# Window attention then top-1 experts: interleaved slots that begin one step later, with routing pieces at other places

## The chip, the cores and the metric

The kernel runs on one core of a Trainium2 chip. The metric is the device time of one execution in microseconds (us). Five engines work side by side, each in its own program order: PE (matrix products, transposes among them), DVE (vector work), ACT (activations and copies), POOL (GpSimd) and SP (which here only issues DMAs). They wait for each other by semaphores.

## What is computed

```python
# q, k, v: 8 batches, 8 heads, 576 positions, 64 wide; window 64; 8 experts, 512 -> 1024 -> 512
scores = q @ k.T / 8, kept where 0 <= i - j < 64
x = softmax(scores) @ v                    # (4608, 512)
logits = x @ w_gate                        # (4608, 8)
e = argmax(logits); gate = softmax(logits)[e]
out = gate * (relu(x @ w1[e]) @ w2[e])     # each row by its one expert
```

All in float32. The expert products are made as three products of split operands (`hi*hi`, `hi*lo`, `lo*hi`), so each weight and each row block is first split into a high and a low part.

## The kernel before

The 4608 rows are 36 tiles of 128. One attention step `i` makes `scores(i)` and, for tiles begun in earlier steps, the exponentials (`exps`, ACT), the transposes of them (`transp`, PE into the bank `t_b`), their copy (`evac`, ACT), the masked halves (`apart`, two products on POOL), the product with v (`values`, PE into `x_b`), the division (`shares`, DVE, then a DMA of the rows to the DRAM table `xs`), the transposes of the finished rows (`rows_t`, PE) and their copy (`cols_t`, ACT tile `xT`). For every second tile, `logits` and in the step after it `by_token` make the router's logits in a spare part of `x_b`; DVE reads them (`lgT`, `lgs`).

Tiles are routed in rounds of 8, 6, 8 and 14 (`ROUNDS`). After a round's last logits, `route` queues eight stages `s1` to `s8` (`slow`); `s4` is the rank product on PE, the others are DVE work. Then come the pieces (`puts`): one `hot_row` a tile, six parts of a table (`here`, `said`), the table's product (`gathered`, PE, and `read`, DVE: `eidx`, `egate`), and the fetches of rows (`early_rows`, indirect DMAs issued by POOL into the three buffers `xg`). Round 1 gives the rows of experts 0 and 1, round 2 those of experts 2 to 7.

The program has four stages:

1. Steps 0 to `TURN - 1` (27 of them), attention alone, written out in one fixed order per step. The last two also turn the two row blocks of expert 0 (`turn`: PE transposes into `m_b`, ACT `xeh`, DVE `xel`).
2. Slots `TURN` to 37: one attention step each, with eight turns (`next(early)`) of the first expert passes between its parts. `first_passes` gives each of the 8 experts two blocks of 128 rows; one of its eight units `j` is 12 products into the hidden bank `m_b` (L280, one turn), with `hh` (ACT), `hl` (DVE) and the splitting of a further weight piece (`whi` ACT, `wlo` DVE), and 6 products of the unit before (L242, `flush`, the other turn). During units 3 and 6 the next expert's rows are turned (units 6 and 7 in expert 1). A slot so holds four units, and two slots an expert.
3. What is left of `early` after the slots, 40 turns; after each of them one step of `steps()`: the last logits, the last round's `s1` to `s8`, the plan of the later passes (`plan`: DVE chains, then the product `want` on PE from `diag`, then the six parts of the big table), `table` (`gathered` with 36 products), and the first fetches. In this stage the hidden banks are `t_b` and `m_b` in turn, and `turn` uses `s_b`.
4. The later passes, two of 384 rows and then nine of 256, and a conditional tail.

PSUM banks are shared: in the slots `t_b` takes `transp`, `rows_t` and `turn` one after the other, each of which waits until ACT (and DVE) have read the one before; `m_b` is the only hidden bank, so the products of unit `j + 1` wait for `hl` of unit `j`.

Of the kernel before, what the change touches and what calls it, by code (L numbers as in the profile page):

```python
# [58 lines left out]
RND = float(1 << 23)  # L59
LOADW = 12  # L60
AHEAD = 2
SPLIT = 16
TURN = 27


CO = {}
# [41 lines left out]
def window_attention_then_top1_moe(ctx: ExitStack, tc: tile.TileContext, qkv, wall, wg, cst, out):  # L108
# [328 lines left out]
    def cols_t(n):  # L437
        q = n % 2
        if q == 0:
            rs_["xT"] = wk.tile([P, 4, 2, P], F32, name="xT", bufs=2)  # L440
        xT = rs_["xT"]
        nc.scalar.copy(out=xT[:, :, q], in_=xps.pop(n).rearrange("p (k t) -> p k t", k=4))
        if q == 1:
            nt = ROUNDS[rs_["round"]]
            if rs_["chunk"] == 0:
                rs_["lgs"] = rt.tile([P, nt, E], F32, name="lgs")
            lgT = rt.tile([P, 2, P], F32, name="lgT")
            c0 = rs_["chunk"]
            rs_["chunk"] += 2
            last = rs_["chunk"] == nt  # L450
            args = nt, rs_["lgs"], rs_["tile0"], rs_["round"]
            lgs = rs_["lgs"]

            def first():
                logits(xT, lgT)

            def second():
                by_token(lgT, lgs[:, c0:c0 + 2], args if last else None)

            rs_["fast"].extend([first, second])  # L460
            if last:
                rs_["tile0"] += nt
                rs_["chunk"] = 0
                rs_["round"] += 1
# [12 lines left out]


    slow, puts = deque(), deque()
    rs_ = {"round": 0, "chunk": 0, "tile0": 0, "fast": deque(), "read": None}  # L480

    def logits(xT, dst):
# [169 lines left out]
    def plan():  # L652
        cnt = small("cnt")
        nc.vector.tensor_tensor(out=cnt, in0=base, in1=cc("ebase"), op=ALU.subtract)
        yield
        nb = floor_of("nb", cnt, 1.0 / P, 127.0 / 256)
        left = small("left")
        nc.vector.tensor_tensor(out=left, in0=nb, in1=cc("st0"), op=ALU.subtract)
        half = floor_of("half", left, 0.5, -0.25)
        odd = stt("odd", half, -2.0, left, ALU.mult, ALU.add)  # L660
        pref = stt("pref", half, 1.0, odd, ALU.is_ge, ALU.mult)
        yield

        ch1 = stt("ch1", running("rk1", pref), float(NWIDE), pref, ALU.is_le, ALU.mult)
        rest = small("rest")
        ts(rest, pref, -1.0, ALU.mult, 1.0, ALU.add)
        sum1 = small("sum1", 1)
        nc.vector.tensor_reduce(out=sum1, in_=ch1, op=ALU.add, axis=AX.X)
        yield
        ok = small("ok")  # L670
        ts(ok, running("rk2", rest), sum1, ALU.add, float(NWIDE), ALU.is_le)
        ch = small("ch")
        nc.vector.tensor_tensor(out=ch, in0=ok, in1=rest, op=ALU.mult)
        nc.vector.tensor_tensor(out=ch, in0=ch, in1=ch1, op=ALU.add)
        yield
        wide = running("wide", ch)
        l2 = stt("l2", ch, float(-WIDE), left, ALU.mult, ALU.add)
        ts(l2, l2, 0.0, ALU.max)
        end = running("end", floor_of("ns", l2, 0.5, 0.25))
        yield  # L680
        nc.vector.tensor_copy(out=tot_sb, in_=end[:, E - 1:E])

        ends = small("ends")
        nc.vector.tensor_tensor(out=ends, in0=wide, in1=end, op=ALU.subtract)
        ends = stt("ends2", ends, cc("kind"), end, ALU.mult, ALU.add)
        yield
        le = small("le")
        ts(le, ends, cc("scol"), ALU.is_le)
        es = small("es", 1)
        nc.vector.tensor_reduce(out=es, in_=le, op=ALU.add, axis=AX.X)  # L690
        yield
        e7 = small("e7", 1)
        ts(e7, es, float(E - 1), ALU.min)
        nc.vector.tensor_copy(out=es_sb, in_=e7)
        nc.vector.tensor_tensor(out=le, in0=le, in1=ends, op=ALU.mult)
        sta = small("sta", 1)
        nc.vector.tensor_reduce(out=sta, in_=le, op=ALU.max, axis=AX.X)
        yield
        begin = stt("begin", ch, cc("three"), cc("st0"), ALU.mult, ALU.add)
        mine = stt("mine", cc("eid"), es, begin, ALU.is_equal, ALU.mult)  # L700
        b0 = small("b0", 1)
        nc.vector.tensor_reduce(out=b0, in_=mine, op=ALU.add, axis=AX.X)
        yield
        blk = small("blk", 1)
        nc.vector.tensor_tensor(out=blk, in0=cc("scol"), in1=sta, op=ALU.subtract)
        blk = stt("blk2", blk, 2.0, cc("ucol"), ALU.mult, ALU.add, 1)
        blk = stt("blk3", es, float(REG), blk, ALU.mult, ALU.add, 1)
        nc.vector.tensor_tensor(out=blk, in0=blk, in1=b0, op=ALU.add)
        ts(blk, blk, NONE, ALU.min)
        yield  # L710

        diag = rt.tile([P, NM], F32, name="diag", bufs=1)
        ts(diag, ident[:, 0:NM], blk, ALU.mult)
        wp = s_b[0][:, 1, 0:NM]
        nc.tensor.matmul(wp, lhsT=ones_f[0:NM], rhs=diag[0:NM], start=True, stop=True)
        want = xn.tile([P, NM], F32, name="want")
        nc.vector.tensor_copy(out=want, in_=wp)
        yield
        keep["want"] = want
        for b in parts(xn, want[:, 0:NMA], NT, NMA):  # L720
            keep["said"] = b
            yield
# [66 lines left out]
    def do_ranks():  # L789
        if slow and slow[0][0]:  # L790
            slow.popleft()[1]()
# [3 lines left out]
            if puts and not slow and (tables or not puts[0][0]):  # L795
                puts.popleft()[1]()

    def do_fast():
        if rs_["fast"]:
            rs_["fast"].popleft()()  # L800
            rs_["read"]()
            rs_["read"] = None

# [14 lines left out]
    def slots(i):  # L818

        if i == TURN:  # L820
            cols_t(i - 5)
            evac(i - 2)
            apart(i - 2)
            turned.append(i - 4)
        each(exps, i - 1)
        back = bool(turned)
        values_shares(i - 3 if i == TURN else i - 2)
        if back:
            move()
        next(early)  # L830
        do_puts(1, False)
        next(early)

        each(transp, i - 1)
        each(evac, i - 1)
        each(apart, i - 1)
        if rs_["fast"]:
            do_fast()
        next(early)
        do_slow(3)  # L840
        do_puts(2)
        next(early)

        move()
        do_ranks()
        next(early)
        do_slow(3)
        do_puts(2)
        next(early)

        if rs_["fast"] and rs_["fast"][0].__name__ == "first":
            do_fast()
        if i == TURN:
            values_shares(i - 2)
        each(scores, i)
        each(folded, i)
        each(largest, i)
        next(early)
        do_slow(1)
        do_puts(1)  # L860
        next(early)

    with tc.manual_schedule():
        for i in range(TURN):
            for c in range(RING, 2 * NS):

                if i == (c - RING + 1) // 2 + 4:
                    nc.sync.dma_start(out=ring[:, c % RING], in_=qkv[c // UC, :, c % UC])
            if i == LOADW:
                ew[0] = Weights(0)  # L870
            if i == SPLIT:
                stream.extend([ew[0].split_(pieces) for _ in range(AHEAD)])
            each(exps, i - 1)
            each(evac, i - 2)
            each(apart, i - 2)
            each(cols_t, i - 5)
            if TURN - 2 <= i < TURN:
                turn(xg[0], i - TURN + 2, xe[0], m_b)
            each(scores, i)
            each(folded, i)  # L880
            each(largest, i)
            each(values, i - 3)
            if rs_["fast"]:
                rs_["fast"].popleft()()
            do_ranks()
            each(rows_t, i - 4)
            each(transp, i - 1)
            each(shares, i - 3)
            if rs_["read"]:
                rs_["read"]()  # L890
                rs_["read"] = None
            do_slow(3)
            do_puts(4)
            if pieces:
                pieces.popleft()()
# [12 lines left out]
        spare["at"] = s_b[0]  # L908

        def steps():  # L910
            do_fast()
            yield
            while slow:
                slow.popleft()[1]()
                yield
            for _ in plan():
                do_puts(1)
                yield
            while puts:
                do_puts(2)  # L920
                yield
            table(0, NMA)
            while keep["turned"] < EARLY - 1:
                yield
            get(0)
            yield
            open_weights(0)
            get(1)
# [71 lines left out]
```

## Time and profile before

| | |
|---|---|
| median of 3 runs | 698.92 us (695.08 to 699.53) |
| profiled execution, its own time | 692.68 us |
| its span | 690.9 us |
| stage 1 (to about 118, with the turned rows to 141) | PE 92.61 of 118 us, then 14.84 of 23 us |
| slots (about 141 to 320) | PE 166.49 of 179 us |
| rest of the first passes (320 to 404) | PE 74.29 of 84 us |
| later passes (404 to 691) | PE 278.31 of 287 us |
| PE, DVE, ACT, POOL over the span | 91%, 63%, 52%, 28% busy |

A busy PE includes the stretches at which the clock granted to it was half, in which the same product takes about twice as long. The granted clock stands in its own column of the views by stretch.

### The profile page before, as it was taken

What the parts mean: (1) busy time and instruction counts of PE and PEld (TensorE: products, weight loads), DVE (VectorE), ACT (ScalarE), POOL (GpSimd) and SP (SyncE); (2) the same over time, 40 slices, a digit from 0 to 9 for tenths busy, and PEclk for the clock granted to TensorE, in tenths of its full rate; (3) what the DMA queues carried; (4) which work ended last, traced back from release to release, by engine and by line L of the source; (5) the groups of instructions that cost most, each with busy time, mean ns of one, the idle gap of its engine ahead of it and who ended that gap; (6) DMA issues with size and microseconds to landing.
All of it is one profiled execution on the core that took longest, in us unless ns stands there. A gap on an engine that the chain in (4) does not pass through costs nothing.

```text
span 690.9 us, 16970 instructions
## 1 busy us (share of the span) xinstructions
PE 626.5 (91%) x6998; PEld 553.4 (80%) x6998; DVE 434.0 (63%) x821; ACT 358.8 (52%) x760; POOL 190.8 (28%) x159
## 2 busy tenths in 40 slices
PE   4897887668996999999987999999999999999995
PEld 3776676557885888887877989999999999999994
DVE  3786989456784857675697554444565556555651
ACT  3664565354653665655444453435655565555551
POOL 2664554531223443311011621112212212110011
PEclk9999999899998999999999999999999999999998
DMA  9788675556372846546454764445666667655520
GB/s 356 248 266 288 243 237 190 187 200 228 126 267 69 300 144 240 189 149 229 132 199 145 246 225 148 161 153 167 219 228 218 212 214 240 210 208 189 205 92 32
DMA packets 32087, 138.13 MB, mean 200 GB/s; under 512 B 4603, under 2 KB 4987, under 8 KB 21633
## 3 DMA queue, kind: packets, MB, share of 16 engines
q1 hardware_dynamic: 25600, 118.08, 49.3%
q0 software_dynamic: 6400, 18.88, 8.1%
q8 instruction: 57, 0.93, 0.5%
q14 instruction: 30, 0.24, 0.1%
HBM read 119.12 MB, written 19.92 MB: 201 GB/s over the span
## 4 chain that ended last, share of the span: by engine, by line
PE 72%; DVE 15%; issue 5%; ACT 4%; DMA 2%; POOL 0%; SPq 0%; ACTq 0%; POOLq 0%; DVEq 0%
PE m_b L280 20%; PE s_b L242 18%; PE t_b L280 11%; PE x_b L242 10%; PE s_b L362 3%; PE x_b L418 3%; DVE wlo L220 3%; DVE mx L377 2%; PE s_b L179 2%; ACT whi L219 1%; DVE s_b L373 1%; ACT pf L388 1%; PE t_b L393 1%; DVE mxs L380 1%; DVE xrow L428 1%
## 5 line engine op out<-in xcount | busy, mean ns | idle before, releaser
L220 DVE TENSOR_TENSOR wlo<-raw,whi 128x1024 fp32r<-128x1024 f32 (+1 forms) x158 | 198.4, 1256 | 142.4 <-ACT whi L219 138.1
L219 ACT CAST whi<-raw 128x1024 fp32r<-128x1024 f32 (+1 forms) x158 | 160.7, 1017 | 75.9 <-PE s_b L242 40.1
L404 POOL TENSOR_TENSOR pm<-tsb,cs 128x512 f32<-128x512 f32 x72 | 91.5, 1293 | 129.8 <-ACT tsb L397 127.2
L286 ACT ACTIVATE hh<-m_b 128x256 fp32r<-128x256 f32 (+1 forms) x98 | 38.6, 394 | 94.0 <-PE m_b L280 94.0
L388 ACT ACTIVATE pf<-s_b,mxs 128x64 f32<-128x64 f32 x288 | 62.9, 333 | 45.2 <-DVE den L424 22.8
L242 PE MATMUL s_b<-whi,hh 128*128 128x512 f32 x208 | 82.4, 396 | 0.0
L242 PE MATMUL s_b<-wlo,hh 128*128 128x512 f32 x208 | 81.9, 394 | 0.0
L242 PE MATMUL s_b<-whi,hl 128*128 128x512 f32 x208 | 81.6, 393 | 0.0
L250 POOL DMA_INDIRECT out<-ys,idx_sb x24 | 30.0, 1251 | 148.9 <-ACT ys L249 145.0
L280 PE MATMUL m_b<-xeh,whi 128*128 128x256 f32 x216 | 65.4, 303 | 0.3 <-DVE hl L287 0.3
L287 DVE SCALAR_TENSOR_TENSOR hl<-m_b,hh 128x256 fp32r<-128x256 f32 (+1 forms) x98 | 42.2, 431 | 37.1 <-ACT hh L286 36.9
L418 PE MATMUL x_b<-ring,pm 64*64 64x65 f32 x2176 | 45.9, 229 | 19.2 <-DVE lgs L471 8.3
L418 PEld LDWEIGHTS x_b<-ring,pm 64*64 64x64 f32 x2176 | 41.6, 141 | 25.4 <-issue 24.6
L280 PE MATMUL m_b<-xel,whi 128*128 128x256 f32 x216 | 61.2, 283 | 0.0
L280 PE MATMUL m_b<-xeh,wlo 128*128 128x256 f32 x216 | 61.1, 283 | 0.0
L280 PE MATMUL t_b<-xh,whi 128*128 128x256 f32 (+1 forms) x176 | 52.3, 297 | 0.0
L280 PE MATMUL m_b<-xh,whi 128*128 128x256 f32 (+1 forms) x176 | 52.3, 297 | 0.0
L168 POOL DMA_INDIRECT xg<-xs,idx_sb x24 | 26.2, 1092 | 93.9 <-PE s_b L179 87.9
L280 PE MATMUL t_b<-xl,whi 128*128 128x256 f32 (+1 forms) x176 | 51.4, 292 | 0.8 <-DVE xl L182 0.8
L280 PE MATMUL m_b<-xh,wlo 128*128 128x256 f32 (+1 forms) x176 | 51.6, 293 | 0.0
L280 PE MATMUL t_b<-xh,wlo 128*128 128x256 f32 (+1 forms) x176 | 51.6, 293 | 0.0
L280 PE MATMUL m_b<-xl,whi 128*128 128x256 f32 (+1 forms) x176 | 51.4, 292 | 0.0
(187 smaller groups left out, 1350.3 us busy)
## 6 DMA issues: line engine op xcount, KB each, us to landing
raw<-wall SPq DMA_DIRECT2D x76, 1024.0 KB, 5.2
ring<-qkv SPq DMA_DIRECT2D x55, 386.0 KB, 4.5
xs<-xrow SPq DMA_DIRECT2D x36, 256.0 KB, 2.3
ring<-qkv SPq DMA_DIRECT2D x5, 1158.0 KB, 11.6
ring<-qkv SPq DMA_DIRECT2D x1, 512.0 KB, 4.0
cs<-cst SPq DMA_DIRECT2D x1, 404.5 KB, 4.5
xg<-xs,idx_sb POOLq DMA_INDIRECT x24, 4.1
out<-ys,idx_sb POOLq DMA_INDIRECT x24, 3.1
```

Of the source, the lines that this page charges most:

```text
L168: nc.gpsimd.indirect_dma_start(out=t[:, u], out_offset=None, in_=xs[0:rows], in_offset=bass.IndirectOffsetOnAxis(ap=ix, axis=0), bounds_ch ...
L219: nc.scalar.copy(out=hi[:, s], in_=raw[:, s])
L220: nc.vector.tensor_tensor(out=lo[:, s], in0=raw[:, s], in1=hi[:, s], op=ALU.subtract)
L242: nc.tensor.matmul(y, lhsT=x[:, us], rhs=w[:, C:], start=(j == 0 and m == 0), stop=(j == NJ - 1 and m == 2))
L250: ins = nc.gpsimd.indirect_dma_start(out=out, out_offset=bass.IndirectOffsetOnAxis(ap=ix, axis=0), in_=ys, in_offset=None, bounds_check=N ...
L280: nc.tensor.matmul(hp[:, 0:w], lhsT=a[:, ks], rhs=x[:, kk, 0:w], start=(m == 0), stop=(m == 11))
L286: nc.scalar.activation(out=hh[:, 0:w], in_=hp[:, 0:w], func=AF.Relu)
L287: nc.vector.scalar_tensor_tensor(out=hl[:, 0:w], in0=hp[:, 0:w], scalar=0.0, in1=hh[:, 0:w], op0=ALU.max, op1=ALU.subtract)
L362: nc.tensor.matmul(sp[cols, a, g], lhsT=q_r[rows, r, g], rhs=k_r[rows, r - 1:r + 1, g], start=True, stop=True)
L388: nc.scalar.activation(out=pf[:, g, a], in_=sp[:, a, g, 0], func=AF.Exp, bias=mx[:, h:h + 1], scale=SCALE)
L404: nc.gpsimd.tensor_tensor(out=pm[i], in0=t.rearrange("p (g q) -> p g q", g=NG), op=ALU.mult, in1=cc("mask")[:, i * P:(i + 1) * P].unsqueez ...
L418: nc.tensor.matmul(x_b[cols, a, g * V1:(g + 1) * V1], lhsT=pm[i][rows, g, cols], rhs=v_r[rows, c % RING - i, g], start=(i == 0), stop=(i = ...
```

## The change

`TURN` and `SPLIT` are one larger: 28 steps come ahead, 10 slots follow, and the rest of the first passes has 48 turns. Inside a slot: the leftover turned rows (`rows_t` of a tile left from the slot before, only in the first two slots) come after the first turn, not ahead of it; `by_token` and `logits` have fixed places, the latter behind `scores`, `folded` and `largest`; the ranks (`s4`) come in the last quarter of the slot, behind the sixth turn; up to ten pieces are put in a slot (2, 3, 3, 2), not six. In the rest: one idle turn ahead of `s4`, two ahead of the product `want`, two ahead of `table`.

```diff
-SPLIT = 16
-TURN = 27
+SPLIT = 17
+TURN = 28
...
-            rs_["fast"].extend([first, second])
+            rs_["fast"].extend([(first, lambda: logits(xT, lgT)),
+                                (second, lambda: by_token(lgT, lgs[:, c0:c0 + 2], args if last else None))])
...
         ts(diag, ident[:, 0:NM], blk, ALU.mult)
+        yield
+        yield
         wp = s_b[0][:, 1, 0:NM]
...
-    def do_fast():
-        if rs_["fast"]:
-            rs_["fast"].popleft()()
+    def do_fast(which):
+        if rs_["fast"] and rs_["fast"][0][0] is which:
+            rs_["fast"].popleft()[1]()
...
         values_shares(i - 3 if i == TURN else i - 2)
+        next(early)
         if back:
             move()
-        next(early)
-        do_puts(1, False)
+        do_puts(2, False)
         next(early)
...
-        if rs_["fast"]:
-            do_fast()
+        do_fast(second)
         next(early)
         do_slow(3)
-        do_puts(2)
+        do_puts(3)
         next(early)
...
         move()
-        do_ranks()
         next(early)
         do_slow(3)
-        do_puts(2)
+        do_puts(3)
         next(early)
...
-        if rs_["fast"] and rs_["fast"][0].__name__ == "first":
-            do_fast()
+        do_ranks()
         if i == TURN:
             values_shares(i - 2)
         each(scores, i)
         each(folded, i)
         each(largest, i)
+        do_fast(first)
         next(early)
-        do_slow(1)
-        do_puts(1)
+        do_slow(2)
+        do_puts(2)
         next(early)
...
         def steps():
-            do_fast()
+            do_fast(second)
             yield
             while slow:
+                if slow[0][0]:
+                    yield
                 slow.popleft()[1]()
                 yield
...
             while puts:
                 do_puts(2)
                 yield
+            yield
+            yield
             table(0, NMA)
```

No instruction of PE, ACT or POOL is added or taken away; the order changes. Three places follow, each before and after.

ACT at the first slot: `pf` are the exponentials, `xT` the copies of turned rows, `tsb` the copy of `transp`. Before:

```order
L442 COPY xT<-m_b 128x4x128
L397 COPY tsb<-t_b 128x512
L388 ACTIVATE pf<-s_b_75,mxs 128x64 x8
L442 COPY xT<-t_b 128x4x128
L286 ACTIVATE hh<-m_b 128x256
L219 CAST whi<-raw 128x1024
```

After:

```order
L503 ACTIVATE ex<-ld 128x64
L442 COPY xT<-m_b 128x4x128
L397 COPY tsb<-t_b 128x512
L388 ACTIVATE pf<-s_b_76,mxs 128x64 x8
L286 ACTIVATE hh<-m_b 128x256
L219 CAST whi<-raw 128x1024
L442 COPY xT<-t_b 128x4x128
```

The copy of the rows turned into `t_b` stood ahead of `hh` and `whi`; it stands behind them, and `ex` of round 2 (`s2`) now stands ahead of the first slot's copies.

DVE where the table of experts 2 to 7 has been read and the rows of expert 2 are turned (`xel`). Before:

```order
L604 TENSOR_TENSOR eidx<-ix_3512,c_tile 128x12
L605 TENSOR_TENSOR egate<-tt_3510 128x12
L606 TENSOR_TENSOR egate<-egate,tt_3510 128x12
L182 TENSOR_TENSOR xel_110<-t_b,xeh_109 128x4x128
L373 COPY_PREDICATED s_b_75<-fold,s_b_75 128x8x64
```

After (each `hl` with the `wlo` behind it is one unit of the expert passes):

```order
L600 TENSOR_TENSOR eidx<-ix_3448,c_tile 128x12
L601 TENSOR_TENSOR egate<-tt_3446 128x12
L602 TENSOR_TENSOR egate<-egate,tt_3446 128x12
L424 TENSOR_SCALAR den<-x_b 128x8
L426 RECIPROCAL rs<-den 128x8
L428 TENSOR_TENSOR xrow<-x_b,rs 128x512
L287 SCALAR_TENSOR_TENSOR hl<-m_b,hh 128x256
L220 TENSOR_TENSOR wlo<-raw,whi 128x1024
L466 TENSOR_REDUCE lgs<-x_b 128x16
```

The turned rows followed the indices at once; now the next `shares` and three units (of which the fence shows the first) come between.

DVE at the plan's product `want` (PE makes `want`'s bank from `diag`; DVE copies it). Before:

```order
L628 TENSOR_SCALAR diag<-cs,blk_5455 128x56
L717 COPY want<-s_b_75 128x56
L570 TENSOR_SCALAR hot_row<-rowb,lo 128x128
L287 SCALAR_TENSOR_TENSOR hl<-t_b,hh 128x256
L220 TENSOR_TENSOR wlo<-raw,whi 128x1024
```

After:

```order
L624 TENSOR_SCALAR diag<-cs,blk_5347 128x56
L566 TENSOR_SCALAR hot_row<-rowb,lo 128x128 x2
L287 SCALAR_TENSOR_TENSOR hl<-m_b,hh 128x256
L220 TENSOR_TENSOR wlo<-raw,whi 128x1024
L715 COPY want<-s_b_75 128x56
```

Nothing stood between `diag` and the copy of its product; now one unit of the expert passes does, on DVE and on PE.

More of the change, by code (lines that the diff above doesn't have):

```diff
@@ L452, in cols_t @@
             lgs = rs_["lgs"]
[L454 to L458, printed above, removed]
-            rs_["fast"].extend([first, second])
+            rs_["fast"].extend([(first, lambda: logits(xT, lgT)),
+                                (second, lambda: by_token(lgT, lgs[:, c0:c0 + 2], args if last else None))])
             if last:
@@ L479, in window_attention_then_top1_moe @@
     slow, puts = deque(), deque()
+    first, second = "logits", "by token"
     rs_ = {"round": 0, "chunk": 0, "tile0": 0, "fast": deque(), "read": None}
@@ L883, in window_attention_then_top1_moe @@
             if rs_["fast"]:
-                rs_["fast"].popleft()()
+                rs_["fast"].popleft()[1]()
             do_ranks()
```

## The prediction

> **What bounds the kernel now.** I read the page first, then the busy time by stage, then the waits of PE, then PE's timeline at each of those waits.
>
> ```profile
> span 690.9 us, 16970 instructions
> ```
>
> ```profile
> core 0: us, PE busy (x) PEld busy (x) DVE busy (x) ACT busy (x) POOL busy (x), PEclk, DMA share, GB/s
> ...
> 118.00:141.00 23.00, 14.84 (x366) 12.66 (x358) 11.22 (x32) 10.33 (x35) 13.23 (x12) 0.85 0.62 192
> 141.00:320.00 179.00, 166.49 (x1983) 145.13 (x1982) 123.04 (x213) 95.46 (x201) 53.54 (x43) 0.97 0.55 191
> 320.00:404.00 84.00, 74.29 (x510) 65.88 (x509) 59.44 (x143) 39.79 (x62) 17.92 (x16) 0.98 0.59 202
> ```
>
> PE is the bound from the first slot on: 166 of 179 us in the slots, 74 of 84 behind them, with DVE at 123 and 59. A change of order leaves PE's work as it is, so what there is to gain is PE's waits in these three stretches, and the half clock that follows them. The waits of PE from 118 to 404 us (who waited for what: total, times, longest):
>
> ```profile
> PE t_b L179 <- DMA xg<-xs,eidx: 5.4, 1, 5.4
> PE m_b L179 <- DMA xg<-xs,eidx: 5.0, 1, 5.0
> PE s_b L715 <- DVE diag L628: 3.9, 1, 3.9
> PE x_b L418 <- DVE lgT L486: 3.4, 2, 2.6
> PE x_b L518 <- DVE oh L513: 2.8, 1, 2.8
> PE s_b L593 <- DVE said L586: 2.6, 1, 2.6
> PE m_b L179 <- ACT xT L442: 1.5, 1, 1.5
> PE t_b L280 <- DVE xel L182: 1.4, 1, 1.4
> PE t_b L435 <- DVE xel L182: 1.4, 1, 1.4
> PE s_b L518 <- DVE oh L513: 1.0, 1, 1.0
> ```
>
> They make 28.4 us in eleven events, none of which recurs from slot to slot. Three are followed by half clock, seen in short windows (PE busy, granted clock):
>
> ```profile
> 157.00:161.00 4.00, 4.00 (x99) 0.71 0.12 41
> 214.00:218.00 4.00, 4.00 (x45) 0.58 0.29 83
> 364.00:368.00 4.00, 4.00 (x18) 0.57 0.62 250
> ```
>
> At these clocks 4.0 us do the work of 2.84, 2.32 and 2.28, so 1.2, 1.7 and 1.7 us are lost there. The first follows an idle time of only 2.6 us (`x_b` for `lgT`). The Trainium skill, "TensorE: Matmul & The Clock Gate", Part 1, says that the clock falls to half after at least one idle window of about 3.4 us. Here the row shows less idle time to be enough, and the row decides.
>
> **The moved step.** PE around the last two steps and the start of slot 27 (start, length, idle before):
>
> ```profile
> 121.28 0.50 PE L593 MATMUL x_b<-said,hot_row 128*128 128x20 bf16 x14 [0.81 <-DVE lgT L486]
> 126.73 1.09 PE L179 MATMUL m_b<-cs,xg 128*128 128x128 f32 x4 [4.96 <-DMA xg<-xs,eidx]
> 127.75 1.99 PE L362 MATMUL s_b<-ring 64*64 64x128 f32 x32
> ...
> 134.51 0.66 PE L179 MATMUL m_b<-cs,xg 128*128 128x128 f32 x4 [1.52 <-ACT xT L442]
> 135.10 1.10 PE L362 MATMUL s_b<-ring 64*64 64x128 f32 x32
> 136.02 1.11 PE L418 MATMUL x_b<-ring,pm 64*64 64x65 f32 x64
> 137.06 0.65 PE L485 MATMUL x_b<-xT,wg_sb 128*32 128x128 f32 x16
> 137.64 0.66 PE L435 MATMUL m_b<-cs,xrow 128*128 128x128 f32 x4
> 138.13 0.60 PE L393 MATMUL t_b<-cs,pf 128*128 128x128 f32 x4
> 139.56 1.16 PE L418 MATMUL x_b<-ring,pm 64*64 64x65 f32 x64 [0.83 <-DVE lgT L486]
> ```
>
> The five rows from 135.10 to 138.73 are one step's attention work at full clock: 3.6 us of PE. One such step leaves the slots, where PE is dense, so the slots lose 3.6 us. It enters ahead of them, at the place where PE stood 4.96 us for the rows of expert 0, because `turn` follows `TURN` and now comes a step later, while the table and the fetch stay. So step 25 begins at 121.8 without a turn. From the scores to the next `turn` lie 6.76 us (127.75 to 134.51), of which 0.9 is the half clock in the scores (1.99 against 1.10): 5.8. The first turn then comes at 127.6, when the rows have landed (126.7); the second 0.6 + 5.8 later, at 134.0; the first slot's `values` 5.05 behind it (134.51 to 139.56), at 139.1. That is 0.4 earlier than now, with a step more done. Both turn steps keep a wait of about 2.3 us for `xT`; I add one half-clock loss of 1.7. Term: -3.6 - 0.4 + 1.7 = **-2.3**. Its ends: without the half clock -4.0; with the whole step as a price, 118 us / 27 = 4.4, and the half clock, +2.5. I take the covered case, since an idle time on PE with nothing else queued is what the step fills. `SPLIT` only moves one split piece from step 16 to 24, and the ring loads on SP keep their steps: nothing.
>
> **The first slot.** ACT there now (start, length):
>
> ```profile
> 139.33 1.75 ACT L388 ACTIVATE pf<-s_b,mxs 128x64 f32<-128x64 f32 x8
> 141.35 0.59 ACT L442 COPY xT<-t_b 128x512 f32<-128x512 f32 x1 [0.27 <-PE t_b L435]
> 142.78 0.38 ACT L286 ACTIVATE hh<-m_b 128x256 fp32r<-128x256 f32 x1 [0.84 <-PE m_b L280]
> 143.06 1.04 ACT L219 CAST whi<-raw 128x1024 fp32r<-128x1024 f32 x1
> ```
>
> Waits removed: `oh` 2.8, because the ranks' `s1` to `s3` now run in step 27 and `s4` three units into the slot; `lgT` 2.6, because no `values` stands right behind `logits` any more; `xel` 1.4 at `rows_t`, which now has a unit ahead of it; `hl` 0.3; and the 1.2 of half clock: -8.3. A new one comes: `rows_t` of the leftover tile now stands between the first unit and `transp`, both in `t_b`, and its `xT` on ACT stands behind `ex`, `xT`, `tsb`, `pf`, `hh` and `whi`. PE: 139.1 + values 1.1 + 12 products 1.5 + `rows_t` 0.45 = 142.2. ACT, from about 139.8, when DVE has read the logits and made `ld` for `ex`: 0.2 + 0.55 + 0.5 + 1.75 + 0.3 + 1.05 + 0.55 = 144.7. So `transp` waits about 2.4, and behind it the whole of PE; with 0.4 more of small waits (`transp` in the next slot) and a half-clock loss of 1.2: +4.0. Term: **-4.3**, between -8.3 (the new wait shorter than the unit) and 0 (all of it back).
>
> **The rows of expert 2.** Now:
>
> ```profile
> 205.89 0.80 PE L593 MATMUL x_b<-said,hot_row 128*128 128x60 bf16 x22
> ...
> 213.56 1.09 PE L179 MATMUL t_b<-cs,xg 128*128 128x128 f32 x4 [5.39 <-DMA xg<-xs,eidx]
> ```
>
> From the table's product to the turned rows 7.7 us pass, with one `flush` between. The units, from the chain of work that ended last:
>
> ```profile
> 185.81 1.43 PE m_b L280 x12
> 187.24 1.39 PE s_b L242 x6
> ```
>
> With ten pieces a slot and experts four units later against the attention, PE then has between the two: `flush` 1.4, `values` 1.1, three units of 2.8 to 2.9, `transp`, `by_token` and `rows_t` 0.9: about 12 us. The wait goes whole, with its half clock: **-7.1**; 5.4 at least. The pieces cost DVE nothing new, they come earlier. POOL issues the fetches ahead of `apart`, whose products `values` needs only a slot later. Next late would be the landing of these rows, with about 4 us to spare.
>
> **The rest.** The slots now end behind the last unit of an expert, not behind a `turn` in `t_b`: -1.4. An idle turn ahead of `s4` is 1.4 us of PE work, against a wait of 1.0: -1.0. Two ahead of `want` are 2.8 against 3.9: 1.1 stays, and the half clock of 1.7 goes. Two ahead of `table` are 2.8 against 2.6: -2.6. Together -1.4 - 1.0 - 2.8 - 1.7 - 2.6 = **-9.5**; if DVE, which has the same work and one unit more in the way, falls behind by half of that, -5. The five turns come from the eight that a slot less leaves over, so the table falls in unit 7 of expert 6, where now it is in unit 1 of expert 7; the fetch has more time, not less.
>
> **The sum.** -2.3 - 4.3 - 7.1 - 9.5 = -23.2; I add 1.2 for small new waits of the pieces (0 to 7.5, see the second rival): -22.0. The profiled execution took 692.7 by its own time (its span and 1.8 around it), so 670.7. The median of the runs, 698.9, lies 6.2 above that execution; the same difference gives **677**. Ends: the best of each term -4.0 - 8.3 - 7.1 - 10.6 (no wait left at `want`) = -30.0, 669; the worst +2.5 - 0 - 5.4 - 5 = -8, 691.
>
> **Rivals.**
> Less is gained: the moved step costs its 4.4 and the first slot's waits come back whole in the new place (`xT`). Against it speaks the 4.96 of idle time; for it, that ACT's queue is long at that place. +2.5 - 7.1 - 5: 689.
>
> The pieces get in the way. DVE and POOL meet in the slots (start, length):
>
> ```profile
> 170.45 1.34 DVE L570 TENSOR_SCALAR hot_row<-rowb,lo 128x128 bf16<-128x128 bf16 x1
> 170.44 2.55 POOL L404 TENSOR_TENSOR pm<-tsb,cs 128x512 f32<-128x512 f32 x2 [22.70 <-ACT tsb L397]
> ```
>
> A piece took 1.34 beside one of POOL's two products. Three pieces right behind `apart` could be held for all 2.5 us and push `hl` back; three slots have pieces: 7.5 at most in place of my 1.2: 683. Against it: DVE has 56 us to spare in the slots. The Trainium skill, "SBUF — State Buffer", Who interferes with whom, says that the second of two such instructions blocks until the first ends; the row agrees.
>
> The clock stays full at the new waits: they are of 2.3 and 2.4 us, and the shortest in the rows above with half clock behind it is 2.6. The losses of 1.7 and 1.2 that I added then don't come: 674. Against it: they follow each other within a few us. By the rule of the Trainium skill's "TensorE: Matmul & The Clock Gate" cited above, it would come out so; the row at 157 speaks against the rule.
>
> Slower: every unit waits for `hl`, as `m_b` is the only hidden bank. From the end of a unit's products `hl` has 1.4 of `flush` and about 0.35 of transposes, 1.75 in all, of which `hh` and `hl` take about 1.1. If DVE's longer queue held `hl` back by 1.4 in all 40 units of the slots, 40 x 0.75 = 30 us come on top: 707. It decides from a delay of 1.2 on. Against it stands how often DVE waits for `hh` now, in the slots:
>
> ```profile
> DVE hl L287 <- ACT hh L286: 27.0, 28, 2.4
> ```
>
> DVE is early in 28 units, by 1 us on average, so the delay would have to be new in all of them.
>
> No change: the waits for DVE and DMA only move one turn on, and the 3.6 of the step alone are gained: 695.
>
> **Chances.** About 1% is what a measurement of this kernel can tell from no change: 692 to 706. The forecast 0.58, the clock 0.12, the pieces 0.10, less gained 0.12, no change 0.05, slower 0.03. Faster is the first four, less 0.02 for the edge of "less gained": 0.90; within 1% 0.07; slower 0.03. The range of 8 in 10 reaches from the best end, 669, to "less gained", 689.
>
> **What would show it.** Right: no PE wait at L179 for `xg` over 1 us; the first slot's `values` near 139 with scores up to 27 done; a wait of `transp` for `xT` of about 2.4 there; the product `want` with about 1 us of wait and no half clock behind it. Wrong: a wait of L280 for `hl` in many units, or the first `values` of the slots at 143 or later.

## The result and the profile after

| | before | changed |
|---|---|---|
| median of 4 runs each | 698.51 us (695.08 to 699.53) | 676.92 us (675.52 to 679.64) |
| ratio to before | | 0.97 (95% interval 0.9676 to 0.9725) |
| profiled execution, its own time | 692.68 us | 679.64 us |

The forecast was 677. The first view is the list of PE's waits in the changed kernel, from round 1's table to the end of the first passes (who waited for what: total, times, longest).

```profile
PE m_b L179 <- DMA xg<-xs,eidx: 3.1, 1, 3.1
PE x_b L418 <- DVE lgs L466: 2.9, 2, 1.7
PE x_b L589 <- DVE lgT L482: 2.3, 2, 1.5
PE t_b L393 <- ACT xT L442: 1.7, 1, 1.7
PE s_b L713 <- DVE diag L624: 1.5, 1, 1.5
PE x_b L418 <- issue: 1.5, 4, 0.4
...
PE m_b L280 <- DVE hl L287: 1.1, 2, 0.8
```

Of the two waits for fetched rows (L179, 5.4 and 5.0 before), one is gone and one has shrunk to 3.1; the waits for `oh` and for the table's part `said` are gone; the wait at `want` (for `diag`, 3.9 before) is 1.5. New are the wait of `transp` for `xT` (L393), waits of `values` for `lgs` (L418; the longest, 1.7, at the first slot's `values`), a wait of 1.5 for `lgT` at the second table product (L589; the other 0.8 was there at the first), and an idle time inside `values` that the profile can't name ("issue").

Eight stretches, cut at the same events in each kernel, show where the time went: 1 ends where round 1's table product starts; 2 at the start of the first expert unit; 3 at that of the fifth; 4 of the twelfth; 5 of the seventeenth (it holds the table and the rows of expert 2); 6 of the thirty-seventh; 7 at the first later pass; 8 at the end. The columns are: borders, length, PE busy (instructions), granted clock, DMA share, GB/s. First a second execution of the kernel before, whose own time of 700.06 lies at the middle of its runs:

```profile
0.00:121.20 121.20, 90.58 (x2502) 0.99 0.75 262
121.20:142.10 20.90, 12.32 (x301) 0.84 0.53 163
142.10:168.30 26.20, 19.84 (x273) 0.87 0.55 200
...
195.60:224.60 29.00, 23.27 (x290) 0.88 0.43 147
...
303.50:408.90 105.40, 96.40 (x697) 0.95 0.54 184
...
```

Then the changed kernel, in the execution that came with the result:

```profile
0.00:122.40 122.40, 92.40 (x2503) 0.97 0.75 258
122.40:144.70 22.30, 15.82 (x403) 0.85 0.62 205
144.70:163.50 18.80, 16.24 (x251) 1.00 0.71 246
163.50:191.90 28.40, 28.02 (x319) 1.00 0.59 204
191.90:219.30 27.40, 24.33 (x306) 0.94 0.51 167
...
296.60:388.70 92.10, 90.33 (x622) 0.98 0.60 207
...
```

Stretch 2 is 1.4 us longer, although it does a whole attention step more (403 instructions against 301). Stretch 3 has lost 7.4, stretch 5 has lost 1.6, and stretch 7 has lost 13.3. In stretch 7, 3.6 of that is the attention work of the step that moved ahead. The table below has the stretches left out here; the later passes (8) are untouched.

Single executions differ, so each kernel was profiled again: twice in all before the change, three times after it. Lengths of the stretches in us, taken between the events themselves and not between rounded borders:

| stretch | before | before again | changed | changed again | changed, third | mean difference |
|---|---|---|---|---|---|---|
| 1 | 121.3 | 121.2 | 122.4 | 122.4 | 123.8 | +1.6 |
| 2 | 19.8 | 20.9 | 22.3 | 22.3 | 23.0 | +2.2 |
| 3 | 25.1 | 26.2 | 18.8 | 18.8 | 18.8 | -6.8 |
| 4 | 27.4 | 27.4 | 28.4 | 28.4 | 28.4 | +1.0 |
| 5 | 27.9 | 29.0 | 27.4 | 26.4 | 22.8 | -2.9 |
| 6 | 78.0 | 78.9 | 77.3 | 77.3 | 77.6 | -1.1 |
| 7 | 102.2 | 105.4 | 92.1 | 92.1 | 90.6 | -12.2 |
| 8 | 289.2 | 289.3 | 289.2 | 289.3 | 289.1 | 0 |
| span | 690.9 | 698.2 | 677.9 | 677.0 | 674.1 | -18.2 |

### The profile page after: what moved, and what is told of

It reads as the page before. It is cut to its first block, busy times and chain, and to the rows that moved or that the text cites. A ratio compares the mean times of both kernels' runs of the same rounds, so it can differ in the third digit from the quotient of the medians.

```text
span 677.9 us, 16980 instructions
## 1 busy us (share of the span) xinstructions
PE 623.4 (92%) x6998; PEld 550.5 (81%) x6998; DVE 430.3 (63%) x821; ACT 359.0 (53%) x760; POOL 190.5 (28%) x159
## 4 chain that ended last, share of the span: by engine, by line
PE 72%; DVE 13%; issue 6%; ACT 5%; DMA 2%; POOL 0%; SPq 0%; ACTq 0%; POOLq 0%; DVEq 0%
PE m_b L280 19%; PE s_b L242 17%; PE t_b L280 11%; PE x_b L242 10%; PE x_b L418 3%; PE s_b L362 3%; DVE wlo L220 3%; ACT pf L388 2%; PE s_b L179 2%; PE t_b L393 1%; DVE mx L377 1%; DVE s_b L373 1%; PE x_b L481 1%; DMA ring<-qkv 1%; DVE xrow L428 1%
## 5 line engine op out<-in xcount | busy, mean ns | idle before, releaser
L242 PE MATMUL s_b<-whi,hh 128*128 128x512 f32 x192 | 76.2, 397 | 0.0
L242 PE MATMUL s_b<-wlo,hh 128*128 128x512 f32 x192 | 75.7, 394 | 0.0
L242 PE MATMUL s_b<-whi,hl 128*128 128x512 f32 x192 | 75.3, 392 | 0.0
L418 PE MATMUL x_b<-ring,pm 64*64 64x65 f32 x2176 | 47.6, 229 | 22.3 <-issue 10.4
L418 PEld LDWEIGHTS x_b<-ring,pm 64*64 64x64 f32 x2176 | 42.2, 140 | 29.2 <-issue 28.2
L280 PE MATMUL m_b<-xeh,whi 128*128 128x256 f32 x208 | 63.2, 304 | 1.1 <-DVE hl L287 1.1
L280 PE MATMUL m_b<-xeh,wlo 128*128 128x256 f32 x208 | 59.2, 285 | 0.0
L280 PE MATMUL m_b<-xel,whi 128*128 128x256 f32 x208 | 59.2, 285 | 0.0
```

The costliest lines, as they stand in the source:

```text
L242: nc.tensor.matmul(y, lhsT=x[:, us], rhs=w[:, C:], start=(j == 0 and m == 0), stop=(j == NJ - 1 and m == 2))
L280: nc.tensor.matmul(hp[:, 0:w], lhsT=a[:, ks], rhs=x[:, kk, 0:w], start=(m == 0), stop=(m == 11))
L418: nc.tensor.matmul(x_b[cols, a, g * V1:(g + 1) * V1], lhsT=pm[i][rows, g, cols], rhs=v_r[rows, c % RING - i, g], start=(i == 0), stop=(i = ...
```

## The experiments

There were two theories. Mine: the time comes from four places, each by its own edit (the step ahead, the places in the first slot, the pieces with the wait for the rows of expert 2, the idle turns). The main rival: fewer of these edits do all the work, or one of them only pushes a wait further along. The runs form three groups, each on one chip with the kernel before beside them, and the ratios go by that.

### The same two kernels again

The kernel before, with nothing edited:

> The kernel before, unchanged, profiled a second time. The profile shown of it took 692.7 us, below all its timed runs (695.1 to 699.5), while the changed kernel's profile, 679.6, is its slowest of four: the two traces differ by 13.0 us, the medians by 21.6. Theory: the trace of before is a fortunate execution, and a second one takes 695 to 700 with 3 to 7 us more of waits or half clock ahead of 404 us. Rival: being profiled costs nothing and the traces are right, then this one is again within 1 us of 692.7 and some 8 us of the medians' difference stay unexplained.

The changed kernel, with nothing edited:

> The changed kernel, unchanged. Theory: 675 to 678, a ratio of 0.97, with the wait for the rows of expert 0 (3.1 us in its first trace, where I had foreseen none) between 0 and 3, as it hangs on when the row fetch lands behind the ring loads. Rival: that wait belongs to the new order; then it is 3 us again.

The kernel before took 700.06; the median of seven runs beside it is 700.13. The changed kernel took 677.94, ratio 0.9675 (0.9633 to 0.9718); PE did not wait for the rows of expert 0 in it, but 2.3 for `xT` at that place, so the wait of 3.1 does not come with the new order each time. The longest waits of the kernel before stood at the same places:

```profile
PE t_b L179 <- DMA xg<-xs,eidx: 5.3, 1, 5.3
PE m_b L179 <- DMA xg<-xs,eidx: 5.1, 1, 5.1
PE s_b L715 <- DVE diag L628: 3.9, 1, 3.9
PE x_b L518 <- DVE oh L513: 2.8, 1, 2.8
```

Each of these four is within 0.1 of the first execution. Others differ by up to 1.1 (`xT` at the turned rows of expert 0 2.6 against 1.5, `lgT` 2.7 against 3.4, `said` 2.0 against 2.6). Yet the span is 7.3 longer. The granted clock makes up most of that. Lost time is the length times what the clock falls short of 1, so in stretches 2, 3, 5 and 7 above it is 20.9 x 0.16 + 26.2 x 0.13 + 29.0 x 0.12 + 105.4 x 0.05 = 15.5. In the first execution the same four stretches read:

```profile
121.30:141.10 19.80, 12.49 (x301) 0.83 0.56 172
141.10:166.20 25.10, 18.05 (x272) 0.93 0.55 207
...
193.50:221.40 27.90, 22.49 (x290) 0.88 0.44 155
...
299.50:401.70 102.20, 93.24 (x695) 0.98 0.54 185
```

They give 3.4 + 1.8 + 3.3 + 2.0 = 10.5. The changed kernel loses 22.3 x 0.15 + 27.4 x 0.06 + 92.1 x 0.02 = 6.8. So some 5.0 of the 7.3 us between two executions of one kernel are the clock, with nearly the same waits. PE's busy time says the same: for the same work it is 5.6 us longer over stretches 2 to 7, and PE's idle time 1.7. Stretch 1 is left out of these sums: the granted clock there was 0.94 in the first execution and 0.99 in the second, at lengths of 121.3 and 121.2, so half clock cost nothing there, where PE is not the bound. Ahead of the last microseconds of the kernel, short windows show the half clock in stretches of 3.4 us or twice that, at places that shift: 155.9 to 159.3 and 210.5 to 217.3 in the first execution, 151.8 to 155.2, 158.6 to 162.0 and 213.2 to 220.0 in the second. The Trainium skill, "TensorE: Matmul & The Clock Gate", Part 1, has the clock follow a free-running window of about 3.4 us, so that one kernel ramps differently from run to run; the traces agree with both points. It also puts the penalty of such ramps below 1% of a usual span; here they took 10.5 of 691 and 15.5 of 698 us, 1.5% and 2.2%, and the measurement decides.

### The step alone

```diff
# in the kernel before
-SPLIT = 16
-TURN = 27
+SPLIT = 17
+TURN = 28
```

> The kernel before with the slots one step later and nothing else. Theory (each wait hangs on its own place): the moved step gives its 3.6 us, the rows of expert 2 come four units earlier against the experts (7.1, by the distance alone), the turned rows at the end of the slots go (1.4), and of the first slot's 8.3 some 4; the waits for oh, diag and said in the rest stay: about 683 against 698.5. Rival (the places and the ten pieces do it, the step gives its PE work alone): 695.

It took 689.08, ratio 0.9817 (0.9763 to 0.9871), in the middle between the theory's 683 and the rival's 695. Its stretch 3 took 18.3 and the wait of 2.8 for `oh` is gone, so all of the first slot's gain is there without the new places. Behind the first slot the waits stay:

```profile
PE t_b L179 <- DMA xg<-xs,eidx: 5.1, 1, 5.1
...
PE s_b L715 <- DVE diag L628: 3.5, 1, 3.5
...
PE s_b L593 <- DVE said L586: 2.1, 1, 2.1
...
PE s_b L518 <- DVE oh L513: 1.0, 1, 1.0
```

The first row settles a reason of mine: the experts stand four units later against the attention here too, and PE still waits 5.1 for the rows of expert 2. The moved step does not remove that wait.

### All but the step

```diff
# in the changed kernel
-SPLIT = 17
-TURN = 28
+SPLIT = 16
+TURN = 27
```

> The changed kernel with the slots beginning where they did before; places, ten pieces and idle turns stay. Theory: the rows of expert 2 still wait some 2 to 5 us, the first slot gains about 3, the rest gains 8 and gives 3 back since the table then comes only two units ahead of the first turned rows of the later passes: about 688 to 691. Rival (the step is not needed): within 1% of the changed kernel, 677 to 683.

It took 684.71, ratio 0.9778 (0.9735 to 0.9821), again between the theory and the rival. The rows of expert 2 are not waited for at L179; those of expert 0 are, as before:

```profile
PE m_b L179 <- DMA xg<-xs,eidx: 5.0, 1, 5.0
```

Stretch 3 took 18.9. So the first slot's gain comes by either edit, and the two gains must not be added. In the medians of this group the step is worth 684.71 - 677.94 = 6.8 on top of the places, and 700.13 - 689.08 = 11.1 by itself.

### Six pieces a slot

```diff
# in the changed kernel
-        do_puts(2, False)
+        do_puts(1, False)
...
-        do_puts(3)
+        do_puts(2)
...
-        do_puts(3)
+        do_puts(2)
...
-        do_slow(2)
-        do_puts(2)
+        do_slow(1)
+        do_puts(1)
```

> The changed kernel with up to six pieces a slot (1, 2, 2, 1), as before. The step alone left the wait for the rows of expert 2 whole (5.1 us), and the ten pieces without the step removed it. Theory: the ranks of round 2 sit in the first slot whether it is step 27 or 28, so only the number of pieces a slot sets the table's unit; the wait comes back with 4 to 6 us and half clock behind it, and the 1.5 us in which the table's product waits for lgT go: 682 to 685 against 677. Rival (the later places of ranks and logits set it): the wait stays away and the time is 676 to 679.

It took 678.06, ratio 0.9695 (0.9652 to 0.9738): no slower than the changed kernel. PE's order explains that, in the timeline (start, length, idle before):

```profile
204.79 0.60 PE L179 MATMUL t_b<-cs,xg 128*128 128x128 f32 x4
209.48 0.79 PE L589 MATMUL x_b<-said,hot_row 128*128 128x60 bf16 x22 [0.88 <-DVE lgT L482]
```

The first row block of expert 2 is turned ahead of the table's product, and so ahead of its own fetch: that block holds other rows than the routed ones, and nothing is waited for. The second block waited 3.7 for its rows. So this run does not price the wait. What it shows is that with ranks in a slot's last quarter six pieces a slot are too few: the table then ends behind the turn that needs it.

### The leftover turned rows first

`transp` waits 1.7 for `xT` because the leftover rows stand between it and the unit. Here they go ahead of the first turn again.

```diff
# in the changed kernel
-        next(early)
         if back:
             move()
+        next(early)
         do_puts(2, False)
```

> The changed kernel with the leftover turned rows ahead of the first turn, as before. Theory: they then wait 0.4 us for the copy of transp, but their own copy stands ahead of the exponentials on ACT again, so the wait of transp falls from 1.7 to 0.6 or less: about 1 us faster, 676. Rival (ACT is the bound at that place, and the wait only moves on to the next unit): no change, within 0.5 us.

It took 677.04, ratio 0.9676 (0.9639 to 0.9714): no change. The wait at `transp` is gone, and others stand in its place ahead of and in the leftover rows:

```profile
PE t_b L435 <- DVE xel L182: 1.2, 1, 1.2
...
PE x_b L418 <- ACT rks L518: 0.7, 1, 0.7
PE t_b L435 <- ACT tsb L397: 0.5, 1, 0.5
```

The wait for `rks` was 0.4 in the changed kernel, so 2.0 is new, and stretch 3 took 19.2, not 18.8. The rival's "no change" came, though what PE waits for in this slot comes from DVE as well as from ACT.

### No idle turns

```diff
# in the changed kernel
         ts(diag, ident[:, 0:NM], blk, ALU.mult)
-        yield
-        yield
...
             while slow:
-                if slow[0][0]:
-                    yield
                 slow.popleft()[1]()
...
-            yield
-            yield
             table(0, NMA)
```

> The changed kernel without its five idle turns in the rest. Theory: PE waits again for oh (1.0), diag (3.9 to 4.4) and said (2.0), with one or two more stretches of half clock: 5 to 8 us slower, 682 to 685. Rival (DVE is as late with the idle turns as without, PE loses the same): within 1.5 us of 677.

It took 686.37, ratio 0.9806 (0.9766 to 0.9846). All three waits came back:

```profile
PE s_b L711 <- DVE diag L624: 3.5, 1, 3.5
...
PE s_b L589 <- DVE said L582: 2.1, 1, 2.1
...
PE s_b L514 <- DVE oh L509: 1.0, 1, 1.0
```

Stretch 7 took 100.1, against a mean of 91.6 with the idle turns. Five turns in which nothing but expert products run are worth 8.5 us: the waits make 6.6 - 1.5 = 5.1 of that, and half clock 2.3 (3.4 lost in stretch 7 of this run, 1.1 on average in the three executions of the changed kernel). The remaining 1.1 has no name.

### Logits first, a third idle turn, ranks earlier, the last turns later

Four attempts at the waits that are left. `logits` right behind the ranks, ahead of `scores`:

```diff
         do_ranks()
+        do_fast(first)
...
         each(largest, i)
-        do_fast(first)
```

> The changed kernel with logits ahead of the scores again (behind the ranks). In the trace the table's product waits 1.5 us for lgT, which DVE reads behind folded and largest, after one of DVE's splits was held 2.3 us by POOL. Theory: lgT is read 1.5 us earlier, that wait goes, and the values of the first slot wait 0.5 to 1 us more for it: 0.5 to 1 us faster, 676 to 677. Rival (DVE is late there as a whole, by the split that POOL held): the wait only shrinks by a third and the values lose as much: no change.

It took 676.05, ratio 0.9673 (0.9636 to 0.9709): not to be told from the changed kernel. The 1.5 for `lgT` at the second table product is gone (the one wait of 0.8 for `lgT` that is left at L589 belongs to the first table product), and new waits of 1.0 (`tt`) and 0.7 (`lgT`) stand at `values`. Its median is 0.9 below that of the changed kernel in the result, less than the intervals can tell.

In the last group the kernel before took 692.28 (689.92 to 694.98 in eleven runs), so only ratios compare with the other groups. The changed kernel stood beside the three edits:

> The changed kernel, unchanged, as the measure for the three beside it. Theory (the runs differ by where the stretches of half clock of 3.4 us fall, not by waits): its waits are those of the first two traces to within 1 us outside the rows of expert 0, and its time is within 3 us of 677. Rival: waits differ by several us from run to run.

674.82, ratio 0.9731 (0.97 to 0.9761). Outside the two turns of expert 0's rows its waits are those of the first two traces to within 1 us, but for `lgs` (1.2, against 2.9 and 1.3) and the idle time inside `values` (none, against 1.5 in both). The ranks ahead of the sixth turn:

```diff
         move()
+        do_ranks()
         next(early)
...
-        do_ranks()
         if i == TURN:
```

> The changed kernel with the ranks (s4) back behind the moved rows, two turns earlier in the slot. Theory: in the first slot oh is long there by then, so the place of the ranks costs and gives nothing by itself once the step has moved; the table of experts 2 to 7 comes a turn or two earlier, and its product no longer stands right behind lgT: the 1.5 us there go, 675 to 677. Rival (the late place is part of the gain): oh or the read of the ranks is waited for again, 678 to 680.

673.18, ratio 0.971 (0.9682 to 0.9738). The table's product now lies in stretch 4 and no longer waits for `lgT`. Stretches 4 and 5 together took 49.3, the least of all kernels, against 51.2 to 55.8 in the changed kernel; but the interval of the ratio overlaps that of the changed kernel. Whether this edit gains 1 to 2 us stays open.

A third idle turn ahead of `want`, with the logits first:

```diff
         ts(diag, ident[:, 0:NM], blk, ALU.mult)
         yield
         yield
+        yield
```

> The changed kernel with logits ahead of the scores again and a third idle turn ahead of the plan's product. Theory: the 1.5 us in which that product waits for diag go, and in most runs the stretch of half clock behind it (1.7): 673 to 675, 1 to 3 us under the changed kernel. Rival (DVE's chain only ends later with one more unit in its way): no change against logits first, 676.

673.68, ratio 0.9725 (0.9702 to 0.9748): no gain. The 1.5 for `diag` is gone, but a turn of rows in the same bank `s_b` now stands directly ahead of the product:

```profile
PE s_b L714 <- DVE xel L182: 2.2, 1, 2.2
```

To that, `turn` of the last two steps behind the ranks in place of ahead of `scores`:

```diff
-            if TURN - 2 <= i < TURN:
-                turn(xg[0], i - TURN + 2, xe[0], m_b)
             each(scores, i)
...
             do_ranks()
+            if TURN - 2 <= i < TURN:
+                turn(xg[0], i - TURN + 2, xe[0], m_b)
             each(rows_t, i - 4)
```

> As third_idle, and in the last two steps ahead of the slots the rows of expert 0 are turned behind the logits, not ahead of the scores. Theory: the two waits of 2.3 us for xT go, and rows_t waits about 1.4 for xel in their place, so each step gets 1 us shorter and a stretch of half clock is less likely: 671 to 673. Rival (the step is bound by DVE and ACT in a chain, PE's place in it is of no weight): within 1 us of third_idle.

675.68, ratio 0.9735 (0.9702 to 0.9767): no gain that can be told. The waits for `xT` in the two turn steps are gone, and others take their place:

```profile
PE m_b L435 <- DVE xel L182: 2.8, 2, 1.4
...
PE x_b L418 <- POOL pm L404: 2.0, 2, 1.1
```

Yet stretch 2 took 20.0 in this trace, against 21.7 with the third idle turn alone, which is nearly the gain of the theory. Stretch 1, which the edit leaves alone, took 126.2 against 121.4, and the trace is the slowest of its six executions (678.59). Whether the edit gains 1 to 2 us stays open here too. None of these versions clearly beats the changed kernel.

## Why the prediction was right, by its steps

The total was right: 677 forecast, 676.92 measured. That it was met to 0.1 us is luck, since two errors cancel: the terms add up to 22.0 where the executions give 18.2, and the 6.2 that I added to come from the profiled execution to the median should have been about 2.5. Each term beside the mean difference of its stretches:

| term | forecast | measured | from |
|---|---|---|---|
| moved step | -2.3 | -1.0 | stretch 2: +2.2, +0.4 for `rows_t`, which moved out of it, -3.6 of attention saved in stretch 7 |
| first slot | -4.3 | -7.2 | stretch 3: -6.8, -0.4 for the `rows_t` that it took in |
| rows of expert 2 | -7.1 | -2.9 | stretch 5 |
| the rest | -9.5 | -8.6 | stretch 7: -12.2, +3.6 of the moved step |
| small new waits | +1.2 | -0.1 | stretches 4 and 6 |
| steps ahead of the change | 0 | +1.6 | stretch 1 |
| sum | -22.0 | -18.2 | |

Between -18.2 and the 21.6 by which the medians differ lie the executions themselves: the two profiled before are on average 2.1 us below the median in the result (own times 692.68 and 700.06 against 698.51), the three after 1.2 above theirs (679.64, 678.74 and 675.83 against 676.92).

**The starting point.** I added the 6.2 us between the profiled execution and the median unexplained. The mean of the two executions before lies 3.7 above the first, and the mean of the three after 1.2 above their median, so 3.7 - 1.2 = 2.5 would have been right by these runs. The second execution before lies 1.5 above the median, and its surplus over the first is mostly half clock (15.5 lost against 10.5). The changed kernel has no such surplus: its profiled execution lies 2.7 above its median. So part of the gain against the typical run is half clock that no longer occurs, mostly in stretches 3, 5 and 7; my sum gave the clock a net of 1.7 only.

**The rows of expert 2** is the step that failed, in its size (2.9 for 7.1) and in one of its reasons. The wait did go whole: the timeline below has the first turned block at 211.80, 16.7 us behind the table's product, without an idle time ahead of it. But stretch 5 gave only 2.9 for it. First, the price left out what DVE does at the place to which the table moves. DVE in the changed kernel, ahead of the table (start, length, idle before):

```profile
186.84 3.64 DVE L220 TENSOR_TENSOR wlo<-raw,whi 128x1024 fp32r<-128x1024 f32 x1 [0.52 <-ACT whi L219]
...
191.77 1.21 DVE L220 TENSOR_TENSOR wlo<-raw,whi 128x1024 fp32r<-128x1024 f32 x1
```

And POOL at that moment:

```profile
186.84 2.55 POOL L404 TENSOR_TENSOR pm<-tsb,cs 128x512 f32<-128x512 f32 x2
```

The split `wlo` takes 1.21 by itself and 3.64 beside POOL's two products, 2.43 more, in all three executions of the changed kernel. The kernel before has the same in the same slot (DVE, then POOL):

```profile
188.69 3.63 DVE L220 TENSOR_TENSOR wlo<-raw,whi 128x1024 fp32r<-128x1024 f32 x1 [0.51 <-ACT whi L219]
```

```profile
188.68 2.54 POOL L404 TENSOR_TENSOR pm<-tsb,cs 128x512 f32<-128x512 f32 x2
```

The Trainium skill, "SBUF — State Buffer", Who interferes with whom, says that a vector instruction with two inputs from SBUF contends with a GpSimd instruction that reads SBUF, and that the one that comes second is blocked until the other ends; the rows agree. So the hold is not new, and that the pieces cost DVE nothing new may stand. What is new is that the table's product comes 8.2 us behind the start of that split, where before it came 17.2 behind it (205.89) and waited for nothing. Behind the held split DVE is busy without a break until `lgT`, and PE's table product waits 1.5 for `lgT`. It takes the order on DVE as well: with the logits ahead of `scores` the hold was as long (3.64) and this wait was gone. The second rival had pieces held and `hl` pushed back in three slots. Here a split of the expert passes is held, and PE waits 0.3 for `hl` behind it. A split takes 3.6 to 3.9 beside POOL in three later slots of both kernels too, and PE waits there for `hl` once at most, 0.8.

Second, PE stands right behind it, in the same `values`:

```profile
195.09 0.79 PE L589 MATMUL x_b<-said,hot_row 128*128 128x60 bf16 x22 [1.51 <-DVE lgT L482]
...
197.29 1.34 PE L418 MATMUL x_b<-ring,pm 64*64 64x65 f32 x51
199.00 0.36 PE L418 MATMUL x_b<-ring,pm 64*64 64x65 f32 x6 [0.37 <-issue]
...
200.47 0.31 PE L418 MATMUL x_b<-ring,pm 64*64 64x65 f32 x1 [0.38 <-issue]
...
211.80 0.60 PE L179 MATMUL t_b<-cs,xg 128*128 128x128 f32 x4
```

From 197.29 to the end at 200.78 it takes 3.5 us; in the third execution the same 64 products go through whole:

```profile
197.13 0.79 PE L589 MATMUL x_b<-said,hot_row 128*128 128x60 bf16 x22 [1.51 <-DVE lgT L482]
...
199.32 1.16 PE L418 MATMUL x_b<-ring,pm 64*64 64x65 f32 x64
...
210.08 0.60 PE L179 MATMUL t_b<-cs,xg 128*128 128x128 f32 x4
```

In that execution 12.95 us lie between the table's product and the turned block (the forecast's "about 12"), and stretch 5 is 22.8, which is 5.6 below the mean before: the forecast's 7.1 less the 1.5 for `lgT`. The two others take 4.6 and 3.6 longer. The slow `values` make 2.3 and 1.7 of that (3.5 and 2.9 against 1.16), and half clock 1.7 in the first; the rest is in smaller pieces. What PE waits for at "issue" no view names; it stays open.

As to the cause of the removed wait, "experts four units later" was wrong: with the step alone 5.1 stayed, and without the step it was gone. What the runs leave is the new places with ten pieces a slot. How much of that is the ten pieces alone stays open, since with six the order itself breaks.

**The first slot** gained 7.2 in place of 4.3. The waits for `oh` and `lgT` and the half clock went as forecast. The new wait of `transp` came, with its cause as forecast (`xT` behind `pf`, `hh` and `whi` on ACT), but 1.7 long, not 2.4, and no half clock followed it: the clock is 1.00 over the whole stretch. That is the third rival's condition at one of its places.

**The moved step** does fill PE's idle time, but the first slot's first `values` stand at 143.5, not at 139.1. PE in the changed kernel:

```profile
122.38 0.50 PE L589 MATMUL x_b<-said,hot_row 128*128 128x20 bf16 x14 [0.81 <-DVE lgT L482]
...
129.89 1.09 PE L179 MATMUL m_b<-cs,xg 128*128 128x128 f32 x4 [3.13 <-DMA xg<-xs,eidx]
...
137.94 0.66 PE L179 MATMUL m_b<-cs,xg 128*128 128x128 f32 x4 [1.24 <-ACT xT L442]
...
143.50 1.16 PE L418 MATMUL x_b<-ring,pm 64*64 64x65 f32 x64 [1.69 <-DVE lgs L466]
```

The table's product itself comes 1.1 later than in the kernel before, at 122.38. The first turn, forecast 6.3 behind the table's product (127.6 against 121.28), comes 7.5 behind it. Here it waited 3.1 for rows that I had counted as landed; in the two other executions it comes 6.6 behind the product and waited not for the rows but 2.3 and 2.9 for `xT`. The second turn follows 8.0 later (8.4 in the two others), not 6.4, and the `values` 5.6 (6.2 and 6.8), not 5.1. So both turn steps keep a wait, as forecast, but the chain from turn to turn is 1.6 to 2.0 longer, which includes half clock (0.85 over stretch 2). My sign that the forecast is wrong, first `values` at 143 or later, occurred (143.5 twice, 145.5 in the third execution); the first slot's surplus paid for it.

**The rest** came within a us: 8.6 against 9.5, and the run without idle turns prices them at 8.5. The wait at `want` is 1.5 against 1.1 forecast. I expected no half clock behind it, and two of the three executions have it. In the first (short window: borders, length, PE busy, clock):

```profile
347.00:351.00 4.00, 4.00 (x20) 0.57 0.75 254
```

The rivals: "slower" by `hl` in every unit did not occur, since PE waits for `hl` twice, 1.1 in all. "No change" and "less gained" did not occur in the total.

**Stretch 1**, 1.6 longer with an order that the change leaves alone there, stays unexplained; the experiments gave 121.4 to 126.2 for it.

## What to carry to other kernels

Where one engine's chain is late, an empty place ahead of its consumer costs nothing as long as other work of the bound engine fills it: five such turns gave 8.5 of some 22 us here. A wait that a new order removes can come back at the next instruction, as it did in several of the later experiments (2.0 in place of 1.7, 2.2 in place of 1.5), so look for the engine that is late there (here DVE and ACT), not only for the wait. Before an event is moved forward, look at what the feeding engine does at its new place. And before one execution is taken as the base of a sum, compare its clock with that of a second one: two executions with nearly the same waits differed by 7 us, 5 of them clock.

## What was not expected of the hardware

A DVE subtraction of two inputs took 3.64 us in place of 1.21 beside two products of POOL that started at the same moment, in the kernel before as well as in the changed one. The clock did not fall behind each wait of like length: in the kernel before it fell at 155.9, 2.0 us into the wait of 2.6 for `lgT`; in the changed kernel it stayed at 1.00 behind 1.7 us at `transp`, and was 0.57 within 2 us of the end of a wait of 1.5 us at `want`; another execution with the same wait there had no half clock in that stretch at all. And 64 small products that take 1.16 us in one execution took 3.5 in another, with three idle times of 0.37 to 0.38 that no releaser explains.
